# Eight experts on lists of chosen tokens instead of on all tokens: 55 tiles of 128 rows, gathered and scattered by DMA

## The chip, the core and the metric

The kernel runs on one core of a Trainium2 chip. The metric is the device time of one execution in microseconds, the median of several runs; lower is better. The core's engines work side by side from their own instruction queues: TensorE (PE, with its weight loads listed apart as PEld), VectorE (DVE), ScalarE (ACT), GpSimd (POOL) and SyncE (SP). SP, ACT and POOL can start DMAs.

## The reference

Two blocks in a row, all in float32: a gated linear recurrence over 768 tokens for each of 4 x 8 heads of 48, and a router that sends each of the 3072 resulting rows x (384 wide) to its two best of eight experts.

```python
for t in range(S):
    state = alpha[:, :, t, :, None] * state + np.einsum('bhd,bhe->bhde', k[:, :, t], v[:, :, t])
    y[:, :, t] = np.einsum('bhd,bhde->bhe', q[:, :, t], state)
# x = y as (3072, 384)
noisy_logits = x @ w_gate + np.log1p(np.exp(x @ w_noise)) * noise
top2 = np.argpartition(-noisy_logits, 2, axis=1)[:, :2]      # weights top2_w: softmax over the two
for e in range(E):
    for k in range(2):
        mask = top2[:, k] == e
        h = np.maximum(x[mask] @ w1[e], 0.0)                  # w1[e]: 384 x 1024
        out[mask] += top2_w[mask, k, None] * (h @ w2[e])      # w2[e]: 1024 x 384
```

## The kernel before

**The recurrence.** The tokens are cut into 24 chunks of 128, six to a batch, and two neighbouring chunks (a pair) run in step. `gla_prepare` loads q, k, alpha and v of a chunk, turns the first three by TensorE transposes (L141, through the PSUM tile `tp`, copied out by ACT or DVE at L142) and forms the diagonal scores. Then seven levels follow (`gla_level`): each makes scores of 4 x 2 heads (`scores`, L148, into `sc`), which DVE copies through a mask into `MT` (L187), while DVE (L197), ACT (L198, L200) and POOL (L199 for `k_new`, L202 for `tot`) scale queries and keys for the next level. `gla_finish` turns the keys (L215), updates the state (L219, L223 to L227), forms y (L233, L238), copies it to `y_sb` (L241) and turns it into `xT` (L246, L247), in which the model dimension lies on the partitions.

**The router.** After every three chunks (a unit of 384 tokens, eight units) `router` makes the logits (L254), the noise, the two best experts and their weights, and writes a dense table `gates`: for each token and expert a weight, which is zero for six of the eight.

**The experts.** `expert(e, u)` runs expert e on all 384 tokens of unit u: eight groups of three matmuls of 384 columns give h (L292, into `h_ps`), ACT takes the Relu (L295), and for each of three chunks eight matmuls of 384 columns give `o_ps` (L301). DVE multiplies by the gate and adds into `acc`, which stays in SBUF for all tokens (L304, L306). The last expert's results go out from there (L308). So all 8 x 8 expert-units are computed, whether a token chose the expert or not. An expert's `w1` and `w2` are loaded once.

**The order.** The recurrence and the router stand under `tc.high_priority()`; expert 0 is written between the pairs and fills TensorE's gaps there. Experts 1 to 7 follow. PSUM has two buffers of each `sc`, one `tp`, one `y` and two for the experts.

## Time and profile before

| | us |
|---|---|
| median of 3 runs (lowest, highest) | 2685.22 (2683.45, 2692.03) |
| span of the profiled execution | 2681.0 |
| PE busy | 2601.9 (97%) |
| PEld, DVE, ACT, POOL busy | 1695.4, 436.9, 461.9, 202.2 |
| L292 and L301, busy | 1047.9 and 1032.3 |
| DMA | 50.52 MB, 19 GB/s on the mean |

The page gives no time outside the span for the profiled execution, so its own time is taken as its span; the median lies 4.2 us above it. Busy time is the union of the instructions' times. A float32 matmul stands in the trace as two instructions (and two weight loads), a transpose as one. An "idle before" names what ended the wait.

### The profile page before, as it was taken

What the parts mean: (1) busy time and instruction counts of PE and PEld (TensorE: products, weight loads), DVE (VectorE), ACT (ScalarE), POOL (GpSimd) and SP (SyncE); (2) the same over time, 40 slices, a digit from 0 to 9 for tenths busy, and PEclk for the clock granted to TensorE, in tenths of its full rate; (3) what the DMA queues carried; (4) which work ended last, traced back from release to release, by engine and by line L of the source; (5) the groups of instructions that cost most, each with busy time, mean ns of one, the idle gap of its engine ahead of it and who ended that gap; (6) DMA issues with size and microseconds to landing.
All of it is one profiled execution on the core that took longest, in us unless ns stands there. A gap on an engine that the chain in (4) does not pass through costs nothing.

```text
span 2681.0 us, 25489 instructions
## 1 busy us (share of the span) xinstructions
PE 2601.9 (97%) x10504; PEld 1695.4 (63%) x10504; DVE 436.9 (16%) x1012; ACT 461.9 (17%) x1005; POOL 202.2 (8%) x412
## 2 busy tenths in 40 slices
PE   7889898999999999999999999999999999999999
PEld 6767677767877655555555555555555555555555
DVE  4333234323544100000000000000000000000000
ACT  2222122222332111111111111111111111111111
POOL 3221022222222000000000000000000000000000
PEclk9975766577777999999999999999999999999999
DMA  7111001111100000010001000000100010000000
GB/s 155 24 21 25 9 19 21 25 24 25 25 16 1 24 24 0 0 47 0 0 0 48 0 0 16 32 0 0 47 0 0 0 48 1 0 1 9 21 21 21
DMA packets 118820, 50.52 MB, mean 19 GB/s; under 512 B 104368, under 2 KB 115632, under 8 KB 118704
## 3 DMA queue, kind: packets, MB, share of 16 engines
q1 hardware_dynamic: 114816, 48.77, 7.3%
q8 instruction: 83, 1.36, 0.2%
q10 hardware_dynamic: 3888, 0.12, 0.1%
q14 instruction: 33, 0.27, 0.0%
HBM read 44.16 MB, written 4.72 MB: 18 GB/s over the span
## 4 chain that ended last, share of the span: by engine, by line
PE 77%; ACT 1%; DVE 0%; issue 0%; ACTq 0%; DVEq 0%
PE h_ps L292 35%; PE o_ps L301 35%; PE sc L148 5%; PE y L238 1%; PE tp L141 1%; PE y L233 0%; PE s L219 0%; PE lg L254 0%; PE tp L215 0%; PE tp L246 0%; DVE q_new L197 0%; ACT L258 0%; DVE q L174 0%; DVE MT L171 0%; ACT tot L142 0%
## 5 line engine op out<-in xcount | busy, mean ns | idle before, releaser
L292 PE MATMUL h_ps<-xT,w 128*128 128x384 f32 x3072 | 1047.9, 498 | 1.7 <-ACT xT L247 1.7
L301 PE MATMUL o_ps<-w,h 128*128 128x384 f32 x3072 | 1032.3, 493 | 0.0
L292 PEld LDWEIGHTS h_ps<-xT,w 128*128 128x128 f32 x3072 | 589.0, 194 | 398.7 <-issue 10.5
L301 PEld LDWEIGHTS o_ps<-w,h 128*128 128x128 f32 x3072 | 583.2, 192 | 392.2 <-issue 4.1
L295 ACT ACTIVATE h<-h_ps 128x384 f32<-128x384 f32 x512 | 251.4, 491 | 1646.4 <-PE h_ps L292 1646.4
L306 DVE SCALAR_TENSOR_TENSOR acc<-o_ps,gates,acc 128x384 f32<-128x384 f32 x168 | 103.8, 618 | 1630.0 <-PE o_ps L301 1630.0
L148 PEld LDWEIGHTS sc<-q_new,k_new 48*128 48x128 f32 x2304 | 258.6, 320 | 51.6 <-issue 26.6
L148 PE MATMUL sc<-q_new,k_new 48*128 48x64 f32 x2304 | 271.3, 412 | 0.0
L187 DVE COPY_PREDICATED MT<-mask,sc 128x256 f32<-128x256 uint32 x336 | 155.0, 526 | 161.0 <-PE sc L148 158.5
L199 POOL TENSOR_TENSOR k_new<-k_new,tot 128x256 f32<-128x256 f32 x144 | 94.2, 656 | 210.0 <-PE sc L148 206.6
L200 ACT COPY k_new<-k_new 128x256 f32<-128x256 f32 x144 | 59.0, 410 | 165.7 <-PE sc L148 148.9
L202 POOL TENSOR_TENSOR tot<-tot 128x256 f32<-128x256 f32 (+6 forms) x168 | 59.8, 356 | 348.4 <-ACT tot L142 281.2
L148 PE MATMUL sc<-q,k 48*128 48x128 f32 (+1 forms) x768 | 75.9, 341 | 8.8 <-DVE MT L171 8.8
L148 PEld LDWEIGHTS sc<-q,k 48*128 48x128 f32 x768 | 69.8, 247 | 15.5 <-DVE MT L171 9.9
L238 PEld LDWEIGHTS y<-vt,MT 128*128 128x128 f32 x384 | 65.2, 256 | 6.3 <-PE s L219 2.3
L238 PE MATMUL y<-vt,MT 128*128 128x48 f32 x384 | 65.0, 333 | 1.9 <-DVE S_bd L223 1.9
L198 ACT COPY q_new<-q_new 128x256 f32<-128x256 f32 x144 | 58.2, 406 | 40.0 <-issue 19.0
L197 DVE TENSOR_TENSOR q_new<-q_new,tot 128x256 f32<-128x256 f32 x144 | 61.1, 439 | 0.0
L141 PE MATMUL tp<-ident,k_in 128*128 128x128 f32 x96 | 23.9, 381 | 20.5 <-DMA k_in<-in_k_dram 11.2
L219 PEld LDWEIGHTS s<-vt,k_end 128*128 128x128 f32 x160 | 30.3, 269 | 15.9 <-ACT k_end L216 11.0
L219 PE MATMUL s<-vt,k_end 128*128 128x96 f32 x160 | 32.0, 359 | 7.4 <-ACT k_end L216 7.4
L233 PE MATMUL y<-S_bd,q_new 128*128 128x96 f32 x160 | 29.6, 342 | 9.5 <-DVE S_bd L227 9.5
(63 smaller groups left out, 521.4 us busy)
## 6 DMA issues: line engine op xcount, KB each, us to landing
w<-in_moe_w_dram SPq DMA_DIRECT2D x16, 1536.0 KB, 6.9
a_in<-in_alpha_dram SPq DMA_DIRECT2D x24, 192.0 KB, 2.7
q_in<-in_q_dram SPq DMA_DIRECT2D x24, 192.0 KB, 2.7
k_in<-in_k_dram SPq DMA_DIRECT2D x24, 192.0 KB, 2.7
vt<-in_v_dram SPq DMA_DIRECT2D x24, 192.0 KB, 2.7
out_dram<-acc SPq DMA_DIRECT2D x24, 192.0 KB, 1.9
noise<-in_moe_noise_dram ACTq DMA_DIRECT2D x1, 96.0 KB, 7.4
w_r<-in_moe_w_gate_dram ACTq DMA_DIRECT2D x1, 12.0 KB, 3.2
```

The lines of the kernel that those rows point to most:

```text
L148: nc.tensor.matmul(sc[i][:, at + j * width:at + (j + 1) * width], kT[r, j, :], qcols[r, j], start=True, stop=True)
L187: nc.vector.copy_predicated(halves(MTs[n % 2][:, i], L)[1], masks[L], part)
L197: nc.vector.tensor_mul(qr_new, q_right, t_left.to_broadcast([C, NP * g, L]))
L199: nc.gpsimd.tensor_tensor(kl_new, k_left, t_right.to_broadcast([C, NP * g, L]), op=ALU.mult)
L200: nc.scalar.copy(kr_new, k_right)
L202: nc.gpsimd.tensor_tensor(tot_new.rearrange("p j g -> p (j g)")[:, :, None], t_left, t_right, op=ALU.mult)
L219: nc.tensor.matmul(s1[:, j], k_end[:, j, :], vt[:, 2 * j:2 * j + 2, :], start=True, stop=True)
L238: nc.tensor.matmul(y[:, h, :], MT[:, i, j, :], vt[:, h, :], start=first and h == 0, stop=h == H - 1, skip_group_check=True)
L292: nc.tensor.matmul(h_ps, w1[:, a, ds(fo * C, C)], xT[:, a, ds(u * UT, UT)], start=a == 0, stop=a == KO - 1)
L295: nc.scalar.activation(h, h_ps, AF.Relu)
L301: nc.tensor.matmul(o_ps, hT[fo][:, ds(c * C, C)], w2[:, fo, :], start=fo == 0, stop=fo == FO - 1)
L306: nc.vector.scalar_tensor_tensor(acc[:, n, :], o_ps, gate, acc[:, n, :], op0=ALU.mult, op1=ALU.add)
```

## The change

The recurrence computes what it did; its PSUM tiles `tp` and `y` get two buffers each, since the experts' PSUM tiles come later. Nothing of the experts is left in that stage. `gla_finish` now also stores each chunk's `y_sb` to DRAM (`x_rows`). `router` no longer writes `gates`: with two small matmuls against triangular and full matrices of ones it counts each token's place in its expert's list, and POOL scatters (token number, weight) pairs of 8 bytes into the DRAM `table` by six indirect DMAs a unit, 48 in all. `out` is set to zero by DMA.

After the recurrence the counts give a `plan`: for each of 55 tiles (48 full ones' worth of 6144 list entries plus 7 for the rounding up of eight lists) the expert and the first table row. The recurrence's pools are closed. Then for every tile SP reads two registers from `plan`, loads 128 table rows (`tab`) and that expert's whole `w1` (`fetch`, two tiles ahead), POOL gathers the 128 rows of x by an indirect DMA, TensorE turns them, h and `o_ps` follow with 128 tokens in place of 384 (TensorE reads the expert number to address `w2`, which lies in SBUF for all experts), POOL gathers the rows that `out` has so far (`prev`), DVE forms weight x o + prev, and POOL scatters the result back to `out`. A list's end is filled with a number beyond the last token, which the indirect DMAs skip.

```diff
+    RMAX = N
+    NTILE = (2 * N) // C + E - 1
+    TROWS = E * RMAX + (E + 0) * C
+    NONE = 2 * N
...
-    ps_sc = pool("ps_sc", 2, space=PS)
-    ps_tp = pool("ps_tp", 1, space=PS)
-    ps_y = pool("ps_y", 1, space=PS)
-    ps_e = pool("ps_e", 2, space=PS)
...
+    ps_sc = pool("ps_sc", 2, gla, space=PS)
+    ps_tp = pool("ps_tp", 2, gla, space=PS)
+    ps_y = pool("ps_y", 2, gla, space=PS)
...
+    x_rows = dram.tile([N, DM], F32, name="x_rows")
+    table = dram.tile([TROWS, 2], U32, name="table")
...
-    def load_expert(e):
-        w1 = w1p.tile([C, KO, F], F32, name="w1")
-        nc.sync.dma_start(out=w1, in_=moe_w1[e].rearrange("(a p) f -> p a f", p=C))
-        w2 = w2p.tile([C, FO, DM], F32, name="w2")
-        nc.sync.dma_start(out=w2, in_=moe_w2[e].rearrange("(a p) d -> p a d", p=C))
-        return w1, w2
...
+    w2 = const.tile([C, E, FO, DM], F32, name="w2")
+    def load_w2():
+        for e in range(E):
+            nc.sync.dma_start(out=w2[:, e], in_=moe_w2[e].rearrange("(a p) d -> p a d", p=C))
...
+        nc.scalar.copy(xT[:, :, ds(at * C, C)], tp[:, 0:KO, :])
+        nc.sync.dma_start(out=x_rows[ds(n * C, C), :], in_=y_sb)
...
+    def router(u, xT):
         lg = ps_y.tile([C, UC, 2, E], F32, tag="y", name="lg")
         for c in range(UC):
             for a in range(KO):
-                nc.tensor.matmul(lg[:, c], xT[:, a, ds((u * UC + c) * C, C)], w_r[:, a],
+                nc.tensor.matmul(lg[:, c], xT[:, a, ds(c * C, C)], w_r[:, a],
...
+        nc.gpsimd.tensor_copy(out=entry.bitcast(I32)[:, :, :, 0],
+                              in_=token[:, ds(u * UC, UC), None].to_broadcast([C, UC, 2]))
...
+        chosen = rp.tile([C, UC, E], F32, name="chosen")
+        nc.vector.tensor_add(chosen, picked[:, 0], picked[:, 1])
+        past = rp.tile([C, UC, E], F32, name="past")
+        nc.vector.tensor_copy(out=past[:, 0], in_=seen[u % 2])
+        for c in range(1, UC):
+            nc.vector.tensor_add(past[:, c], past[:, c - 1], chosen[:, c - 1])
+        nc.vector.tensor_add(seen[(u + 1) % 2], past[:, UC - 1], chosen[:, UC - 1])
+        rank = ps_y.tile([C, UC, E], F32, tag="y", name="rank")
+        nc.tensor.matmul(rank, before, chosen, start=True, stop=False)
+        nc.tensor.matmul(rank, ones, past, start=False, stop=True)
...
+        place_u = rp.tile([C, 2 * UC], U32, name="place_u")
+        nc.vector.tensor_copy(out=place_u, in_=place_f)
         for c in range(UC):
-            n = u * UC + c
-            o_ps = ps_e.tile([C, DM], F32, tag="e", name="o_ps")
-            for fo in range(FO):
-                nc.tensor.matmul(o_ps, hT[fo][:, ds(c * C, C)], w2[:, fo, :], start=fo == 0, stop=fo == FO - 1)
-            gate = gates[:, n, e:e + 1]
-            if e == 0:
-                nc.vector.tensor_scalar(out=acc[:, n, :], in0=o_ps, scalar1=gate, scalar2=None, op0=ALU.mult)
-            else:
-                nc.vector.scalar_tensor_tensor(acc[:, n, :], o_ps, gate, acc[:, n, :], op0=ALU.mult, op1=ALU.add)
-            if e == E - 1:
-                nc.sync.dma_start(out=out[ds(n * C, C), :], in_=acc[:, n, :])
-    # ---- the recurrence, two chunks in step, and the router go first; the first expert fills their gaps ----
-    weights = None
+            for k in range(2):
+                i = k * UC + c
+                nc.gpsimd.indirect_dma_start(
+                    out=table, out_offset=bass.IndirectOffsetOnAxis(ap=place_u[:, i:i + 1], axis=0),
+                    in_=entry.bitcast(U32)[:, c, k, :], in_offset=None)
...
     for n in range(0, NT, 2):
-        with tc.high_priority():
-            pair = {m: gla_prepare(m) for m in (n, n + 1)}
-            for L in LEVELS:
-                for m, c in pair.items():
-                    gla_level(m, c, L)
+        pair = {m: gla_prepare(m) for m in (n, n + 1)}
+        for L in LEVELS:
             for m, c in pair.items():
-                gla_finish(m, c)
+                gla_level(m, c, L)
+        for m, c in pair.items():
+            if m // UC not in xTs:
+                xTs[m // UC] = xtp.tile([C, KO, UT], F32, name="xT")
+            gla_finish(m, c, xTs[m // UC], m % UC)
         if n == 0:
             load_router()
-            weights = load_expert(0)
+            for i in range(8):
+                nc.sync.dma_start(out=out.rearrange("(i n p) d -> i p n d", i=8, p=C)[i], in_=zeros)
+        if n == 2:
+            load_w2()
         while (done + 1) * UC <= n + 2:
-            with tc.high_priority():
-                router(done)
-            expert(0, done, *weights)
+            router(done, xTs.pop(done))
             done += 1
-    for e in range(1, E):
-        weights = load_expert(e)
-        for u in range(NU):
-            expert(e, u, *weights)
...
+    total = ps_y.tile([C, E], F32, tag="y", name="total")
+    nc.tensor.matmul(total, ones, seen[NU % 2], start=True, stop=True)
+    total_sb = rp.tile([1, E], F32, name="total_sb")
+    nc.vector.tensor_copy(out=total_sb, in_=total[0:1, :])
...
+    plan = const.tile([1, NTILE, 2], I32, name="plan")
+    nc.vector.tensor_copy(out=plan[:, :, 0], in_=of)
+    nc.vector.tensor_copy(out=plan[:, :, 1], in_=first)
...
+    def fetch(i):
+        e = nc.values_load(plan[0:1, i, 0:1], engines=[mybir.EngineType.SP], min_val=0, max_val=E - 1,
+                           skip_runtime_bounds_check_because=WHY)
+        r = nc.values_load(plan[0:1, i, 1:2], engines=[mybir.EngineType.SP], min_val=0, max_val=TROWS - C,
+                           skip_runtime_bounds_check_because=WHY)
+        tab = tp_.tile([C, 2], U32, name="tab")
+        nc.sync.dma_start(out=tab, in_=table[ds(r, C), :])
+        w1 = w1p.tile([C, KO, F], F32, name="w1")
+        nc.sync.dma_start(out=w1, in_=moe_w1[ds(e, 1)].rearrange("o (a p) f -> p (o a) f", p=C))
+        nc.gpsimd.indirect_dma_start(out=x_in[i % NB], out_offset=None, in_=x_rows,
+                                     in_offset=bass.IndirectOffsetOnAxis(ap=tab[:, 0:1], axis=0),
+                                     bounds_check=N - 1, oob_is_err=False)
+        return tab, w1
+    def ffn(i, tab, w1):
+        e = nc.values_load(plan[0:1, i, 0:1], engines=[mybir.EngineType.PE], min_val=0, max_val=E - 1,
+                           skip_runtime_bounds_check_because=WHY)
+        x_ps = ps_x.tile([C, KO, C], F32, name="x_ps")
+        for a in range(KO):
+            nc.tensor.transpose(x_ps[:, a, :], x_in[i % NB][:, ds(a * C, C)], ident)
+        xt = xp.tile([C, KO, C], F32, name="xt")
+        nc.vector.tensor_copy(out=xt, in_=x_ps)
+        h = hp.tile([C, FO, C], F32, name="h")
+        for half in range(2):
+            h_ps = ps_h.tile([C, FO // 2, C], F32, name="h_ps")
+            for fo in range(FO // 2):
+                for a in range(KO):
+                    nc.tensor.matmul(h_ps[:, fo, :], w1[:, a, ds((half * FO // 2 + fo) * C, C)], xt[:, a, :],
+                                     start=a == 0, stop=a == KO - 1)
+            nc.scalar.activation(h[:, ds(half * FO // 2, FO // 2), :], h_ps, AF.Relu)
+        o_ps = ps_o.tile([C, DM], F32, name="o_ps")
+        for fo in range(FO):
+            nc.tensor.matmul(o_ps, h[:, fo, :], w2[:, ds(e, 1), fo, :].rearrange("p o d -> p (o d)"),
+                             start=fo == 0, stop=fo == FO - 1)
+        nc.gpsimd.indirect_dma_start(out=prev[i % 2], out_offset=None, in_=out,
+                                     in_offset=bass.IndirectOffsetOnAxis(ap=tab[:, 0:1], axis=0),
+                                     bounds_check=N - 1, oob_is_err=False)
+        o = op.tile([C, DM], F32, name="o")
+        nc.vector.scalar_tensor_tensor(o, o_ps, tab.bitcast(F32)[:, 1:2], prev[i % 2], op0=ALU.mult, op1=ALU.add)
+        nc.gpsimd.indirect_dma_start(out=out, out_offset=bass.IndirectOffsetOnAxis(ap=tab[:, 0:1], axis=0),
+                                     in_=o, in_offset=None, bounds_check=N - 1, oob_is_err=False)
+    ahead = [fetch(0), fetch(1)]
+    for i in range(NTILE):
+        if i + 2 < NTILE:
+            ahead.append(fetch(i + 2))
+        ffn(i, *ahead[i])
```

How the instructions now stand, at the places on which the prediction rests. TensorE in the expert stage before, from one unit's last h group through its three o groups (`w` are the weights, an entry is one float32 matmul or several alike):

```order
L292 MATMUL h_ps<-xT,w_8585 128x384 [waits Activation_49]
L292 MATMUL h_ps<-xT,w_8585 128x384 x2
L301 MATMUL o_ps<-w_8587,h 128x384 [waits Activation_49]
L301 MATMUL o_ps<-w_8587,h 128x384 x6
L301 MATMUL o_ps<-w_8587,h 128x384 [waits Activation_49]
L301 MATMUL o_ps<-w_8587,h 128x384 x8
L301 MATMUL o_ps<-w_8587,h 128x384 [waits DVE_49]
L301 MATMUL o_ps<-w_8587,h 128x384 x7
```

TensorE in the tile stage now, from the transposes of two tiles to the first o matmul of the first of them (TENSOR_LOAD reads the register, ISA forms the address):

```order
L429 MATMUL x_ps<-ident,x_in_5727 128x128 [waits DMASW6_49]
L429 MATMUL x_ps<-ident,x_in_5727 128x128 x2
L429 MATMUL x_ps<-ident,x_in_5728 128x128 [waits DMASW1_49]
L429 MATMUL x_ps<-ident,x_in_5728 128x128 x2
L437 MATMUL h_ps<-xt,w_9103 128x128 [waits DMAHW3_49,DVE_49]
L437 MATMUL h_ps<-xt,w_9103 128x128 x11
L437 MATMUL h_ps<-xt,w_9103 128x128 [waits PE_49]
L437 MATMUL h_ps<-xt,w_9103 128x128 x11
L425 TENSOR_LOAD plan
L442 ISA
L442 MATMUL o_ps<-w_189,h 128x384 [waits Activation_49]
L442 ISA
```

The transposes of two tiles stand together, ahead of the first one's h; the h of every second tile follows the o of the tile before it directly.

VectorE at the end of the program before, and in the tile stage now:

```order
L304 TENSOR_SCALAR acc<-o_ps,gates 128x384 [waits PE_49] x3
L304 TENSOR_SCALAR acc<-o_ps,gates 128x384 [waits DVE_49,PE_49]
L304 TENSOR_SCALAR acc<-o_ps,gates 128x384 [waits PE_49] x2
L306 SCALAR_TENSOR_TENSOR acc<-o_ps,gates,acc 128x384 [waits PE_49] x18
L306 SCALAR_TENSOR_TENSOR acc<-o_ps,gates,acc 128x384 [waits DVE_49,PE_49] x150
```

```order
L431 COPY xt<-x_ps 128x384 [waits DVE_49,PE_49] x2
L448 SCALAR_TENSOR_TENSOR o<-o_ps,tab,prev_5731 128x384 [waits DMASW7_49,DMASW3_49,DMAHW2_49,DVE_49,PE_49]
L448 SCALAR_TENSOR_TENSOR o<-o_ps,tab,prev_5730 128x384 [waits DMASW6_49,DMASW2_49,DMAHW4_49,DVE_49,PE_49]
L431 COPY xt<-x_ps 128x384 [waits DVE_49,PE_49] x2
L448 SCALAR_TENSOR_TENSOR o<-o_ps,tab,prev_5731 128x384 [waits DMASW5_49,DMASW1_49,DMAHW6_49,DVE_49,PE_49]
```

The two copies that TensorE's next h waits for stand behind the sum of the tile before, and that sum waits for a gather (DMASW).

POOL in the middle of a pair's levels before, and at the like place now (`tot` and `k_new` of two chunks alternate), then POOL in the tile stage, where before there was nothing:

```order
L199 TENSOR_TENSOR k_new<-k_new,tot_1749 128x128x2 [waits PE_49]
L199 TENSOR_TENSOR k_new<-k_new,tot_1769 128x128x2 [waits PE_49]
L199 TENSOR_TENSOR k_new<-k_new,tot_1787 128x64x4 [waits PE_49,Activation_49,Pool_49]
L199 TENSOR_TENSOR k_new<-k_new,tot_1805 128x64x4 [waits PE_49,Activation_49,Pool_49]
L199 TENSOR_TENSOR k_new<-k_new,tot_1825 128x32x8 [waits PE_49,Activation_49,Pool_49]
```

```order
L338 DMA table<-entry,place_u 25600x2 [waits DVE_49]
L224 TENSOR_TENSOR k_new<-k_new,tot_1674 128x128x2 [waits PE_49]
L224 TENSOR_TENSOR k_new<-k_new,tot_1694 128x128x2 [waits PE_49]
L338 DMA table<-entry,place_u 25600x2 [waits DMASW6_49]
L224 TENSOR_TENSOR k_new<-k_new,tot_1712 128x64x4 [waits PE_49,Activation_49,Pool_49]
L224 TENSOR_TENSOR k_new<-k_new,tot_1730 128x64x4 [waits PE_49,Activation_49,Pool_49]
```

```order
L449 DMA out_dram<-o,tab 3072x384 [waits DMASW4_49,DVE_49]
L444 DMA prev_5731<-out_dram,tab 128x384 [waits DMASW7_49,DMASW6_49]
L419 DMA x_in_5727<-x_rows,tab 128x384 [waits DMAHW6_49,PE_49]
L449 DMA out_dram<-o,tab 3072x384 [waits DMASW7_49,DVE_49]
L444 DMA prev_5730<-out_dram,tab 128x384 [waits DMASW2_49,DMASW1_49]
```

In the recurrence one scatter now stands between two levels, and each waits for the scatter ahead of it (DMASW). In the tile stage a tile's gather of `prev` waits for the scatter of the tile before, since both touch `out`.

## Rows read from the trace of the kernel before

**Rows 1.** The page: engine totals, PE in 40 slices, granted clock.

```profile
PE 2601.9 (97%) x10504; PEld 1695.4 (63%) x10504; DVE 436.9 (16%) x1012; ACT 461.9 (17%) x1005; POOL 202.2 (8%) x412
...
PE   7889898999999999999999999999999999999999
...
PEclk9975766577777999999999999999999999999999
```

**Rows 2.** Stretches: length, busy per engine (instructions), granted clock, DMA share, GB/s.

```profile
0.00:943.50 943.50, 868.00 (x5128) 674.16 (x5129) 332.49 (x843) 241.90 (x557) 202.17 (x412) 0.75 0.14 29
943.50:2681.00 1737.50, 1733.94 (x5377) 1021.25 (x5375) 104.40 (x169) 220.04 (x448) 0.00 (x0) 1.00 0.04 13
11.17:72.46 61.29, 52.74 (x350) 47.09 (x350) 24.70 (x54) 15.59 (x38) 15.95 (x30) 1.00 0.65 151
...
30.00:40.00 10.00, 10.00 (x95) 9.95 (x95) 7.42 (x18) 4.30 (x12) 3.89 (x6) 1.00 1.04 388
```

**Rows 3.** The page's groups: busy us, mean ns of one, idle before.

```profile
L292 PE MATMUL h_ps<-xT,w 128*128 128x384 f32 x3072 | 1047.9, 498 | 1.7 <-ACT xT L247 1.7
L301 PE MATMUL o_ps<-w,h 128*128 128x384 f32 x3072 | 1032.3, 493 | 0.0
```

**Rows 4.** Timeline of the last units: start, length, instruction, idle before.

```profile
2615.36 15.64 PE L292 MATMUL h_ps<-xT,w 128*128 128x384 f32 x48
...
2630.84 15.64 PE L301 MATMUL o_ps<-w,h 128*128 128x384 f32 x48
...
2646.32 15.64 PE L292 MATMUL h_ps<-xT,w 128*128 128x384 f32 x48
...
2677.48 0.62 DVE L306 SCALAR_TENSOR_TENSOR acc<-o_ps,gates,acc 128x384 f32<-128x384 f32 x1 [4.54 <-PE o_ps L301]
```

**Rows 5.** Timeline of the first two pairs, which run without expert work.

```profile
11.17 1.09 PE L141 MATMUL tp<-ident,k_in 128*128 128x128 f32 x4 [11.17 <-DMA k_in<-in_k_dram]
12.93 1.11 PE L141 MATMUL tp<-ident,q_in 128*128 128x128 f32 x4 [0.68 <-ACT k L142]
...
28.23 17.49 PE L148 MATMUL sc<-q_new,k_new 48*128 48x64 f32 x158
...
35.65 0.64 POOL L199 TENSOR_TENSOR k_new<-k_new,tot 128x256 f32<-128x256 f32 x1 [1.23 <-PE sc L148]
...
54.57 3.62 PE L238 MATMUL y<-vt,MT 128*128 128x48 f32 x16 [0.93 <-DVE S_bd L223]
...
60.32 1.09 PE L215 MATMUL tp<-ident,k_new 128*128 128x128 f32 x4 [0.66 <-ACT xT L247]
...
72.46 1.12 PE L141 MATMUL tp<-ident,k_in 128*128 128x128 f32 x4 [0.57 <-ACT xT L247]
...
123.45 17.27 PE L292 MATMUL h_ps<-xT,w 128*128 128x384 f32 x48 [0.57 <-ACT xT L247]
```

**Rows 6.** Timeline just behind the first expert work, through the first router.

```profile
150.88 0.60 PE L215 MATMUL tp<-ident,k_new 128*128 128x128 f32 x4
...
155.21 1.91 PE L238 MATMUL y<-vt,MT 128*128 128x48 f32 x16
...
157.69 2.18 PE L254 MATMUL lg<-w_r,xT 128*128 128x16 f32 x18 [0.57 <-ACT y_sb L241]
...
163.55 0.16 DVE L274 TENSOR_TENSOR den<-w 128x3 f32<-128x3 f32 x1 [0.16 <-ACT w L272]
```

**Rows 7.** DMA issues: instructions, KB each, median us from issue to landing.

```profile
w<-in_moe_w_dram SPq DMA_DIRECT2D x16, 1536.0 KB, 6.9
...
out_dram<-acc SPq DMA_DIRECT2D x24, 192.0 KB, 1.9
noise<-in_moe_noise_dram ACTq DMA_DIRECT2D x1, 96.0 KB, 7.4
```

**Rows 8.** All groups of instructions: the shortest kind on POOL.

```profile
L347 POOL MEMSET const-float32-1.0<- 128x1 f32 x1 | 0.1, 99 | 0.0
```

More of the change, by code (lines that the diff above doesn't have):

```diff
@@ L83 @@
         g = C // (2 * L)
-        m = const.tile([C, g, L], F32, name=f"mask{L}")
+        m = gc.tile([C, g, L], F32, name=f"mask{L}")
         nc.gpsimd.memset(m, 1.0)
@@ new lines @@
+    ends = rp.tile([1, E], F32, name="ends")
+    nc.vector.tensor_tensor_scan(ends, ones[0:1, 0:E], tiles, 0.0, op0=ALU.mult, op1=ALU.add)
+    behind = rp.tile([1, NTILE, E], F32, name="behind")
+    nc.vector.tensor_tensor(behind, tile_no[:, :, None].to_broadcast([1, NTILE, E]),
+                            ends[:, None, :].to_broadcast([1, NTILE, E]), op=ALU.is_ge)
+    of = rp.tile([1, NTILE], F32, name="of")
+    nc.vector.reduce_sum(out=of, in_=behind, axis=mybir.AxisListType.X)
+    nc.vector.tensor_mul(behind, behind, tiles[:, None, :].to_broadcast([1, NTILE, E]))
@@ new lines @@
+    for t in x_in + prev:
+        nc.gpsimd.memset(t, 0.0)
+    WHY = "computed from the counts, in range by construction"
+    def fetch(i):
[11 more added lines that the diff above has]
+        return tab, w1
```

120 lines of the change are left out of this document (79 added, 41 removed).

## The prediction

> **What bounds the kernel now.** I read the page's totals and slices first: TensorE is busy 97% of the span, without a gap in the last two thirds, while POOL is done after them [rows 1]. Then the stretches: the seven experts from 943.5 us on hold TensorE for 1733.9 of 1737.5 us at granted clock 1.00, with the DMA engines at 4% [rows 2]. The groups say whose time it is: L292 and L301 are 2080 us of the 2681 [rows 3]. The last units show that nothing else matters there: h and o follow each other every 15.48 us (2615.36, 2630.84, 2646.32), so one expert on one unit of 384 tokens is 30.96 us, and seven experts on eight units are 56 x 30.96 = 1734 us [rows 4]. That stage is pure matmul, and six of every eight token-expert pairs in it are multiplied by zero. The stage ahead of it, 943.5 us, is the recurrence with expert 0 in its gaps, at clock 0.75 on the mean.
>
> What the recurrence is by itself stands at the start, before any expert work is ready: the first pair goes from 11.17 to 72.46, 61.3 us, of which TensorE is busy 52.7 [rows 2, 5]. The granted clock reads 1.00 there, but no change of it is recorded yet, and the same work says otherwise: four transposes take 1.09 us in it and 0.60 just behind the first expert unit, the 16 matmuls of L238 3.62 and 1.91 [rows 5, 6]. So the recurrence alone runs at the lower level, 1.2 GHz, though TensorE is busy 10.00 of 10 us in its levels [rows 2]; expert work before it is what brought the higher one.
>
> **The change part by part. Removed:** all of expert 0 to 7 on all tokens, 64 x 30.96 = 1981 us of full-clock TensorE time.
>
> **Stage one, the recurrence without expert work.** Three pairs of a batch: 61.3 us; 63.1 (72.46 to 123.45, and a second finish like 60.32 to 72.46 behind it); about 58.7 for the third, whose last chunk has no state to update (transposes 1.09, matmuls and two waits, some 4.4 in all) [rows 5]. That is 183 a batch, 732 for four. The second buffers of `tp` and `y` take away the waits for one buffer: 0.68 and its like twice a chunk, 0.93, 0.66 and 0.57 in the finish [rows 5]; the first pair's idle time is 61.3 - 52.7 = 8.6, and I count 5.5 of it as gone, 66 in all. With the 11.2 us before the first transpose: 677. The work that could hide in those gaps (expert 0) is gone, so nothing is won or lost by it beyond this.
>
> The router comes on top. The logits, 2.18 us at the higher level [rows 6], are about 4.1 at the lower; two counting products are four instructions more, about 0.9; and TensorE meets a wait for the chain of ACT and VectorE, which took from 157.69 + 2.18 to 163.55, 3.7 us, to the sum of the weights [rows 6], behind which the list of chosen experts now stands. TensorE's order has other work ahead of the counting product at most boundaries; I take 2 of it. Eight units x 7 = 56: stage one 733.
>
> 48 scatters now stand in POOL's queue between the `k_new` of one level and the next; queued behind each are the keys that TensorE's next scores need. POOL waits 1.23 us for TensorE ahead of each 0.64 us of `k_new` [rows 5], twice a level, so one scatter of up to 2.4 us in a level is covered by that wait. No row shows an indirect DMA. Its nearest rows are the store of 192 KB in the same 1536-byte rows, 1.9 us to landing, and, as the costliest for its size, 96 KB in 3072 pieces, 7.4 us [rows 7]. At 1.9 the scatters are free; at 7.4, each waiting for the one before, 48 x 5 = 240 us. I take 0.4 us each, 19: stage one ends at **752** (bounds 733 and 973).
>
> **Between the stages** one thing follows another: 6 us from the last logits through places and counts; six scatters in a row, each waiting for the one before (3 us each, 18; bounds 11 and 44); the table rows, then the gather beside the first `w1`, 6.9 us [rows 7], 9; transposes and copy, 2. Sum **35** (28 to 61). TensorE has stood still by then, so the first tile starts at the lower level: **4** more.
>
> **Stage two, 55 tiles.** An o product has the same eight matmuls of 384 columns as before, a third of 15.48: 5.16 us [rows 4]. The h product has 24 matmuls of 128 columns in place of 384. By columns that is 5.16; but each instruction also loads 128x128 weights, and where the columns are few (48) the pitch is 1.91 / 16 = 0.119 us [rows 6], by which 48 instructions would be 5.7. I take 5.4. Three transposes are 3/4 of 0.60, 0.45 [rows 6]. Sum 11.0.
>
> Two waits come on top. For every second tile, the copies of two turned tiles stand on VectorE behind the sum of the tile just finished: 0.62 for the sum [rows 4] and about as much for the copy, 0.4 in hand-offs, less the 0.9 of transposes that run meanwhile: 0.7, or 0.4 a tile. And the register with the expert number is read between h and o. No row shows such a read; it lies between nothing (the queue behind it still busy) and the 1.9 us of the shortest transfer [rows 7]; 0.8, nearer to nothing, since a read moves 4 bytes. A tile is 12.2 us, 55 are **671** (bounds 11.0 and 14.0: 605 and 770). The Trainium skill's page DMA: Bandwidth & Descriptors (Latency and other measured facts) gives such a read a floor of about 600 ns; by that the stage would be 11 us shorter, 660, which no run here shows yet.
>
> What hides the DMAs: the sum of one tile must be scattered before the next tile's `prev` may be gathered, and that must land before the next sum. From sum to sum this chain is 0.6 + scatter + gather; at 3.5 us each (nearer to the 1.9 us row, as it has the same rows and bytes, but with software descriptors and beside the loads of `w1`) it is 7.6, under the 11.4 to 12.9 us that TensorE needs from one o to the next: 3.8 us of cover, gone when a transfer passes 5.4. The gather of x is issued two tiles ahead. `w1` now comes 55 times, 1536 KB each with 6.9 us to land [rows 7], some 1.5 tiles ahead; with three row transfers of 192 KB that is 2.16 MB in 12.2 us, 177 GB/s, where 388 were reached [rows 2]. **The tail**: a last sum and scatter, 4.
>
> Sum: 752 + 35 + 4 + 671 + 4 = 1466, and 4 us by which the median lies above the span: **1470 us**.
>
> **The rivals.** *The chain through `out` sets the tile.* If an indirect transfer is nearer to the 7.4 us of many pieces [rows 7], from sum to sum it is 0.6 + 7.4 + 7.4 + 0.4 = 15.8, TensorE waits in every tile, and stage two is 869; with 50 more for the scatters in stage one and 26 more between the stages, about 1740. For it: 128 pieces each, generated by POOL, beside 16 engines' worth of `w1`; against: half the bytes' rows are as long as those of the 1.9 us store.
>
> *The tiles run at 1.2 GHz.* TensorE then needs about 2 x 11.0 + 1.2 = 23.2 a tile, 1276, in all about 2075. For it: the levels of the recurrence are all busy and stay at the lower level. Against: 128 rows by 128 and 384 columns are the experts' own kind of work, which holds 1.00 for 1737 us [rows 2], and the waits I find are about 1 us.
>
> *The recurrence gets the higher level.* Its TensorE work would halve, to 26 us a pair, the waits stay: 35 x 12 + 11 + 45 = 476 in place of 752, about 1195 in all. Rows speak against it: two pairs of it alone, 112 us, stayed at the doubled durations [rows 5]. The Trainium skill's page TensorE: Matmul & The Clock Gate (Part 1) has it that sustained matmul activity releases the throttle, and by that rule this case would come; the durations here disagree for TensorE work of this kind, at least before.
>
> *Slower: POOL writes the row addresses one by one.* If each of 128 rows costs about what POOL's shortest instruction takes, 99 ns [rows 8], an indirect transfer holds POOL for 12.7 us, three make a tile 38 us, and stage two is 2096; the 48 scatters, 10 us each beyond their cover, add 490 to stage one: about 3340. It decides from 165 transfers and 48 scatters reaching the 1890 us between 795 and 2685, that is from about 9.4 us each, 73 ns a row. Against it: the nearest row with many pieces, 3072 in 7.4 us [rows 7], is 2.4 ns a piece.
>
> *The change doesn't do what it says*, in that the 55 tiles are fixed: the seven for rounding cost full price (already in the sum, 85 us) and cannot cost more.
>
> **How the numbers follow.** Forecast, tiles set by TensorE at the higher clock: 0.62, with its own range 1400 to 1600 (bounds of register read, scatters and the middle). Chain through `out`: 0.22, 1600 to 1850, mostly below 1760. Tiles at 1.2 GHz: 0.07. Recurrence at 2.4 GHz: 0.05. Slower: 0.02; the rest scatters. The range to hold 8 in 10 is 1370 to 1760. A change under 0.3% is about what a measurement of this kernel can't tell from none: faster 0.97, same 0.01, slower 0.02.
>
> **What the profile after would show.** Right: a recurrence that ends near 750 us, its L173 at the durations of [rows 5]; 55 tiles at a pitch of 12 us with o at 5.2 and h at 5.4; granted clock 1.00 in them; VectorE's sum waiting for TensorE, not for a DMA. Wrong: the sum waiting for `prev` (the chain), h at twice 5.4 (the clock), POOL busy through a tile (row by row), or a gap of over 60 us between the stages.

## The result, and the profile after

The changed kernel takes 1466.8 us (median; 1463.9 to 1474.7) where the kernel before takes 2688.0; the ratio is 0.5464, 95% interval 0.5446 to 0.5482. The forecast was 1470 us. The profiled execution spans 1462.2 us, 4.6 less than the median.

From the page, first the totals, then the span in 40 slices (36.6 us each), as in [rows 1]:

```profile
PE 1241.1 (85%) x8079; PEld 1071.5 (73%) x8079; DVE 394.7 (27%) x985; ACT 274.5 (19%) x603; POOL 425.4 (29%) x653
...
PE   6895697997979979699850999989999989999896
...
PEclk8655555555555555555555999999999999999999
```

TensorE's busy time has gone from 97% to 85%, and the two stages are plain to see: the recurrence at half clock (0.5, the lower level of 1.2 GHz) up to slice 21, one slice in which TensorE does almost nothing, then the tiles at full clock. The stretches have the columns of [rows 2]:

```profile
10.05:755.60 745.55, 629.78 (x4394) 585.22 (x4394) 325.42 (x852) 208.60 (x493) 242.19 (x425) 0.55 0.25 55
...
755.00:800.00 45.00, 0.64 (x4) 0.55 (x3) 4.67 (x18) 0.00 (x0) 9.19 (x9) 0.50 0.17 61
...
800.02:1451.25 651.23, 611.30 (x3685) 486.23 (x3685) 61.92 (x110) 65.67 (x110) 163.62 (x161) 0.99 0.49 173
```

So the time is 755.6 + 44.4 + 651.2 + 11.0 us for the recurrence, the middle, the tiles and the tail, against 752 + 35 + 675 + 4 (671 and the 4 of the first tile) in the prediction. What TensorE waits for shows where its 15% went (waiting engine and line, releaser: us in all, times, longest):

```profile
PE x_ps L429 <- DMA x_in<-x_rows,tab: 81.8, 26, 44.4
PE sc L173 <- POOL k_new L224: 41.4, 13, 20.8
PE tp L240 <- POOL k_new L224: 31.1, 6, 8.7
...
PE h_ps L437 <- DVE xt L431: 1.7, 3, 0.7
```

In the recurrence TensorE waits 72.5 us (41.4 and 31.1) for keys (`k_new`) that stand on POOL behind the table scatters; 20.8 of it is one wait, behind the first unit's scatters. In the tiles it waits 37.4 us (81.8 less the 44.4 of the middle) for the gather of x. The scatters' own groups say why the keys are late:

```profile
L338 POOL DMA_INDIRECT table<-entry,place_u x48 | 48.7, 1015 | 176.9 <-DMA table<-entry,place_u 106.2
```

```profile
L338 POOL DMA_INDIRECT table<-entry,place_u x48: 957/1006/1364, 123.0 to 785.6; - x48
...
DMA to landing us min/median/max: 4.5/5.2/9.0
```

POOL spends 1.0 us on each, and each waits until the one before has landed (its data has arrived), 5.2 us from its issue on the median. The middle is a row of six of them, from the timeline (start, us, what, idle time before and its releaser):

```profile
755.07 0.57 PE L366 MATMUL total<-seen,ones 128*128 128x8 f32 x2
...
756.95 1.36 POOL L338 DMA_INDIRECT table<-entry,place_u  x1 [30.04 <-DVE ends L376]
...
763.32 0.96 POOL L338 DMA_INDIRECT table<-entry,place_u  x1 [5.00 <-DMA table<-entry,place_u]
...
785.59 0.96 POOL L338 DMA_INDIRECT table<-entry,place_u  x1 [4.58 <-DMA table<-entry,place_u]
790.41 0.36 SPq L416 DMA_DIRECT2D tab<-table  x1
...
800.02 0.90 PE L429 MATMUL x_ps<-ident,x_in 128*128 128x128 f32 x3 [44.37 <-DMA x_in<-x_rows,tab]
...
801.62 8.21 PE L437 MATMUL h_ps<-xt,w 128*128 128x128 f32 x48 [0.70 <-DVE xt L431]
```

Two tiles on TensorE and the start of the next two, as [rows 4] showed the units before. The order is the transposes of two tiles, then the two tiles; 23.49 us for two (1008.64 to 1032.13), 11.84 a tile on the mean of 55:

```profile
1006.50 0.49 PE L429 MATMUL x_ps<-ident,x_in 128*128 128x128 f32 x3
1008.26 0.55 PE L429 MATMUL x_ps<-ident,x_in 128*128 128x128 f32 x3 [1.27 <-DMA x_in<-x_rows,tab]
1008.64 5.52 PE L437 MATMUL h_ps<-xt,w 128*128 128x128 f32 x48
1014.00 5.33 PE L442 MATMUL o_ps<-w,h 128*128 x16
1019.17 5.52 PE L437 MATMUL h_ps<-xt,w 128*128 128x128 f32 x48
1024.52 5.33 PE L442 MATMUL o_ps<-w,h 128*128 x16
1029.69 0.49 PE L429 MATMUL x_ps<-ident,x_in 128*128 128x128 f32 x3
1031.75 0.55 PE L429 MATMUL x_ps<-ident,x_in 128*128 128x128 f32 x3 [1.57 <-DMA x_in<-x_rows,tab]
1032.13 5.52 PE L437 MATMUL h_ps<-xt,w 128*128 128x128 f32 x48
```

An h is 5.36 us from its start to that of o, an o 5.17 to the next h: 10.53 a tile. The gather of x costs 1.27 and 1.57 before every second tile. Two waits, of SP and of POOL, lead to it:

```profile
SPq L416 <- DMA out_dram<-o,tab: 504.7, 52, 23.4
...
POOL x_in L419 <- DMA tab<-table: 59.8, 44, 3.9
```

SP may load the next table rows only when a scatter of sums has landed, and POOL waits for these rows before it issues the gather. Behind the scatter issued at 1020.27 the table rows follow at 1023.09, the gather at 1025.54, the transposes at 1031.75. These are the second tile's transposes, which TensorE's order has ahead of the first tile's products: the rows of x are needed a whole tile before the second tile's own h. No run here tries the other order.

### The profile page after: what moved, and what is told of

Its sections match the earlier page's. It is cut to its first block, busy times and chain, and to the rows that moved or that the text cites. A ratio compares the mean times of both kernels' runs of the same rounds, so it can differ in the third digit from the quotient of the medians.

```text
span 1462.2 us, 21684 instructions
## 1 busy us (share of the span) xinstructions
PE 1241.1 (85%) x8079; PEld 1071.5 (73%) x8079; DVE 394.7 (27%) x985; ACT 274.5 (19%) x603; POOL 425.4 (29%) x653
## 5 line engine op out<-in xcount | busy, mean ns | idle before, releaser
L437 PEld LDWEIGHTS h_ps<-xt,w 128*128 128x128 f32 x2640 | 308.5, 196 | 10.1 <-DVE xt L431 2.9
L437 PE MATMUL h_ps<-xt,w 128*128 128x128 f32 x2640 | 311.3, 279 | 1.8 <-DVE xt L431 1.7
L173 PE MATMUL sc<-q_new,k_new 48*128 48x64 f32 x2304 | 268.2, 418 | 42.0 <-POOL k_new L224 41.4
L173 PEld LDWEIGHTS sc<-q_new,k_new 48*128 48x128 f32 x2304 | 257.9, 327 | 53.0 <-POOL k_new L224 44.6
L442 PE MATMUL o_ps<-w,h 128*128 x880 | 292.9, 486 | 0.0
L442 PEld LDWEIGHTS o_ps<-w,h 128*128 128x128 f32 x880 | 163.2, 190 | 101.8
L448 DVE SCALAR_TENSOR_TENSOR o<-o_ps,tab,prev 128x384 f32<-128x384 f32 x55 | 34.0, 618 | 559.7 <-PE o_ps L442 496.3
L439 ACT ACTIVATE h<-h_ps 128x512 f32<-128x512 f32 x110 | 65.7, 597 | 626.7 <-PE h_ps L437 626.7
L449 POOL DMA_INDIRECT out_dram<-o,tab x55 | 56.4, 1026 | 306.7 <-DVE o L448 294.4
L338 POOL DMA_INDIRECT table<-entry,place_u x48 | 48.7, 1015 | 176.9 <-DMA table<-entry,place_u 106.2
L429 PE MATMUL x_ps<-ident,x_in 128*128 128x128 f32 x165 | 28.9, 287 | 81.8 <-DMA x_in<-x_rows,tab 81.8
L444 POOL DMA_INDIRECT prev<-out_dram,tab x55 | 56.4, 1026 | 112.3 <-DMA out_dram<-o,tab 108.6
L419 POOL DMA_INDIRECT x_in<-x_rows,tab x55 | 54.8, 996 | 79.4 <-DMA tab<-table 59.8
```

The source lines that it names most:

```text
L173: nc.tensor.matmul(sc[i][:, at + j * width:at + (j + 1) * width], kT[r, j, :], qcols[r, j], start=True, stop=True)
L419: nc.gpsimd.indirect_dma_start(out=x_in[i % NB], out_offset=None, in_=x_rows, in_offset=bass.IndirectOffsetOnAxis(ap=tab[:, 0:1], axis=0), ...
L437: nc.tensor.matmul(h_ps[:, fo, :], w1[:, a, ds((half * FO // 2 + fo) * C, C)], xt[:, a, :], start=a == 0, stop=a == KO - 1)
L439: nc.scalar.activation(h[:, ds(half * FO // 2, FO // 2), :], h_ps, AF.Relu)
L442: nc.tensor.matmul(o_ps, h[:, fo, :], w2[:, ds(e, 1), fo, :].rearrange("p o d -> p (o d)"), start=fo == 0, stop=fo == FO - 1)
L444: nc.gpsimd.indirect_dma_start(out=prev[i % 2], out_offset=None, in_=out, in_offset=bass.IndirectOffsetOnAxis(ap=tab[:, 0:1], axis=0), bou ...
```

## The experiments

Each changes the kernel after. Stages are read from its profiled run: up to the start of the product that counts the entries (`total`), from there to the first turned tile, to the end of the last sum, and from there to the end (the tail). Stage one of the same code came out between 755 and 767 us in seven kernels (762 on the mean, and 755.1 in the changed kernel is the shortest), the tiles of the same code between 641 and 652, so a difference under 10 us in one stage of one run says little.

| kernel | median, us | ratio to before, interval | stage one | middle | tiles | tail |
|---|---|---|---|---|---|---|
| after | 1466.8 | 0.5446 to 0.5482 | 755.1 | 44.9 | 651.2 | 11.0 |
| expert 0's register | 1465.8 | 0.5442 to 0.5476 | 764.4 | 44.7 | 642.1 | 11.0 |
| single PSUM buffers | 1530.1 | 0.5694 to 0.5718 | 830.9 | 45.0 | 641.5 | 11.0 |
| six tables | 1391.8 | 0.5179 to 0.5198 | 714.5 | 24.3 | 637.2 | 11.0 |
| deeper fetch | 1448.0 | 0.5384 to 0.5402 | 758.1 | 45.6 | 632.4 | 11.0 |
| deeper, copies on ScalarE | 1439.3 | 0.5326 to 0.5378 | 764.4 | 44.7 | 616.3 | 10.9 |
| deeper, two gathers | 1584.5 | 0.5867 to 0.5917 | 766.6 | 44.0 | 766.2 | 6.8 |
| deeper, ScalarE, two gathers | 1500.1 | 0.5568 to 0.5596 | 760.4 | 44.6 | 691.5 | 6.9 |
| deeper, six tables | 1377.2 | 0.5111 to 0.5138 | 706.2 | 24.9 | 633.8 | 11.0 |
| deeper, six tables, ScalarE | 1370.8 | 0.5080 to 0.5115 | 712.6 | 23.8 | 622.1 | 10.9 |
| scores over 64 rows | 1461.7 | 0.5427 to 0.5461 | 755.7 | 44.0 | 646.9 | 11.0 |
| scores over 128 rows | 1481.7 | 0.5488 to 0.5549 | 780.7 | 43.7 | 651.0 | 11.0 |
| no last scatter | 1464.8, one run | none | 763.4 | 44.8 | 652.1 | 2.7 |

**The register read.**

```diff
-        e = nc.values_load(plan[0:1, i, 0:1], engines=[mybir.EngineType.PE], ...
+        e = 0
...
-            nc.tensor.matmul(o_ps, h[:, fo, :], w2[:, ds(e, 1), fo, :]...
+            nc.tensor.matmul(o_ps, h[:, fo, :], w2[:, e, fo, :],
```

> TensorE reads no register: every tile takes the second product's weights from expert 0 (a part of the computation that is changed), all else is as in the changed kernel. By the prediction's term, 0.8 us a tile, the time falls by 44 us to 1423. By the trace, where the read takes 0.30 us while the queued products of h still run and o starts 5.36 us after h without a gap, nothing changes: within 4 us of 1467.

1465.8 us: no change. (Its tiles, 642.1, are as long as the 641.5 of the kernel with single buffers, which reads the register.) The read, in the changed kernel (min/median/max ns, first and last start):

```profile
L425 PEldq TENSOR_LOAD <-plan x55: 299/303/489, 807.7 to 1443.3; - x55
```

0.30 us while the queued products of h still run: an o starts 5.36 us after its h, as steadily as the next h after the o. The prediction's 0.8 a tile, 44 us, was put on a read that the queued products cover. The Trainium skill's page DMA: Bandwidth & Descriptors (Latency and other measured facts) has a floor of about 600 ns for such a read, twice what this trace shows; since the read is hidden, neither figure counts here.

**The second PSUM buffers.**

```diff
-    ps_tp = pool("ps_tp", 2, gla, space=PS)
-    ps_y = pool("ps_y", 2, gla, space=PS)
+    ps_tp = pool("ps_tp", 1, gla, space=PS)
+    ps_y = pool("ps_y", 1, gla, space=PS)
```

> The PSUM pools for turned tiles and for sums have one buffer each again, as before the change. By the prediction's term, 5.5 us a pair, the time rises by 66 us to 1533. By the idle time of the first pair, 8.6 us before and 4.4 after, it is 4.2 a pair, 50 us, less what the scatters' waits swallow: 1500 to 1517.

1530.1 us, 63 more. By the traces it is 76 more in stage one (69 against the mean of the seven kernels) and 10 less in the tiles, whose code is the same. The prediction's 66 is about right, its mechanism only in part; the 1500 to 1517 us from idle time alone were too low. The recurrence with single buffers, to be read against the first stretch above (745.55 us, TensorE busy 629.78):

```profile
10.05:831.50 821.45, 674.55 (x4394) 609.46 (x4394) 326.57 (x854) 208.88 (x493) 238.17 (x425) 1.00 0.21 50
```

(The clock column reads 1.00 as in [rows 2]: no change is recorded in this stretch; durations are those of the lower level, 423 ns on the mean for the score products read from `q` and `k`, where the changed kernel has 333.) Of 76 us, 31 are waits (146.9 against 115.8 us idle). The other 45 are the same 4394 instructions running longer (against the mean of the seven, 28 and 41). In the changed kernel the end of one pair and the preparation of the next stand close together on TensorE, and there the granted clock goes up for a few microseconds, once in most pairs:

```profile
446.10:450.00 3.90, 3.90 (x30) 3.14 (x30) 1.14 (x2) 1.65 (x3) 0.34 (x1) 0.67 0.64 153
450.00:454.60 4.60, 3.69 (x44) 3.07 (x44) 4.03 (x8) 2.59 (x6) 3.90 (x10) 1.00 0.99 165
...
460.00:470.00 10.00, 9.95 (x94) 9.80 (x93) 6.82 (x18) 4.46 (x14) 4.85 (x8) 0.50 0.01 2
```

With single buffers TensorE waits some 0.9 us between the steps of that block (21.7 us in 24 waits for the copy of `k`, 17.2 in 20 for that of `q`), and the higher level doesn't come: the durations there stay those of the lower one.

**The 48 table scatters.** Six tables, so that no scatter waits for another:

```diff
-    table = dram.tile([TROWS, 2], U32, name="table")
+    tables = [dram.tile([TROWS, 2], U32, name=f"table{i}") for i in range(6)]
...
-                    out=table, out_offset=...
+                    out=tables[i], out_offset=...
...      the filling of the empty tables, now behind the first pair:
-    nc.scalar.dma_start(out=table...
+            for t in tables:
+                nc.scalar.dma_start(out=t...
...
-        tab = tp_.tile([C, 2], U32, name="tab")
-        nc.sync.dma_start(out=tab, in_=table[ds(r, C), :])
+        six = tp_.tile([C, 6, 2], U32, name="six")
+        for s in range(6):
+            nc.sync.dma_start(out=six[:, s], in_=tables[s][ds(r, C), :])
+        tab = tp_.tile([C, 2], U32, name="tab")
+        nc.vector.tensor_reduce(out=tab[:, 0:1], in_=six[:, :, 0], op=ALU.min, axis=...)
+        nc.vector.tensor_reduce(out=tab.bitcast(F32)[:, 1:2], in_=six.bitcast(F32)[:, :, 1], op=ALU.max, axis=...)
```

> Six tables in place of one, one for each of the six scatters of a unit, so that no scatter has to wait for the one before; a tile reads its rows from all six and takes the smallest row number and the largest weight. Theory (a scatter takes 5.2 us to land, and as each waits for the one before on POOL, the keys of the next levels stand behind them; the waits of TensorE for these keys were 72.5 us): stage one falls from 754 to 690 to 710 us, and between the stages six scatters take 6 + 5 us in place of 34, so that gap falls from 45 to 22 to 26; the time is 1375 to 1405. Rival (POOL's own time for 48 scatters, 1.0 us each, and the work of landing are what costs): stage one stays above 730, only the gap shrinks, 1430 to 1445.

1391.8 us, inside the theory's range: stage one 714.5, a little above what it gave, the middle 24.3. What is left of the waits for keys (with 6.9 us "issue" in the same group):

```profile
PE sc L172 <- POOL k_new L223: 13.4, 4, 7.7
...
PE sc L172 <- issue: 6.9, 4, 2.8
```

```profile
142.96 0.51 POOL L249 TENSOR_TENSOR S_bd<-S_bd,tot 48x192 f32<-48x192 f32 x1 [7.23 <-DMA table<-entry,place_u]
```

The longest, 7.7 us, stands in the first unit, where POOL waits 7.2 us for the scatters to land before it scales the state (`S_bd`). Most of the rest is POOL's own time: six scatters of 1.0 us follow each other directly. The three kernels with six tables have stage one at 706 to 715 us (711 on the mean, against 762 for the seven with one table), so the chain of scatters costs about 50 us there and 20 of the 45 in the middle.

**The gather of x.** First the fetch three tiles ahead, then also the copies on ScalarE:

```diff
-    tp_ = pool("tabp", 3)
+    tp_ = pool("tabp", 5)
-    NB = 3
+    NB = 5
-    ahead = [fetch(0), fetch(1)]
+    ahead = [fetch(0), fetch(1), fetch(2)]
-            ahead.append(fetch(i + 2))
+            ahead.append(fetch(i + 3))
...  second kernel:
-        nc.vector.tensor_copy(out=xt, in_=x_ps)
+        nc.scalar.copy(xt, x_ps)
```

> Three to five buffers for the gathered rows and for the table rows, and the rows of a tile fetched three tiles ahead in place of two. The changed kernel's trace has TensorE wait 37 us in stage two for the gather of x (81.8 us in 26 waits, less the 44.4 before the first tile), about 1.5 us before every second tile. Theory (the table rows have only three buffers, so the gather of a tile starts when the sum of the tile three before it has landed, and comes just too late): these waits go, stage two falls from 651 to about 615 us, the time to 1425 to 1437. Rival (the waits come from POOL's order, each gather standing behind the scatter and the gather of the tile in hand): within 10 us of 1467.

> The deeper fetch, and the copies of the turned rows on ScalarE in place of VectorE. With the deeper fetch alone (1448 us) TensorE no longer waits for the gather of x but 22.2 us for these copies, which stand behind the sum on VectorE. Theory: they need not stand there; the wait falls below 8 us, the time to 1428 to 1436. Rival (the hand-off costs as much from ScalarE, whose copy of the same tile is 0.5 us): within 5 us of 1448.

1448.0 us: half of the gain that was expected. The gather of x is no longer waited for in the tiles (45.0 us, the middle alone), and SP's wait of 504.7 us for the scatters is gone, as the theory has it; buffers and distance were changed together, so their shares are not told apart. But another wait shows that this one had covered, in the deeper-fetch kernel's group:

```profile
L437 PE MATMUL h_ps<-xt,w 128*128 128x128 f32 x2640 | 311.4, 279 | 22.2 <-DVE xt L431 22.2
```

These 22.2 us are the 0.4 a tile that the prediction had for the copies behind the sum on VectorE. With the copies on ScalarE they are 8.5 us and the tiles take 616.3, 35 less than after, where the two waits held 39. The time, 1439.3, misses the expected range by 3 us (in the profiled run stage one is 6 us longer than with the deeper fetch alone); the interval (0.5326 to 0.5378) lies below that of the deeper fetch alone.

**The chain through `out`.** On top of each of the last two kernels, `prev` is gathered twice:

```diff
         nc.gpsimd.indirect_dma_start(out=prev[i % 2], out_offset=None, in_=out, ...)
+        nc.gpsimd.indirect_dma_start(out=prev[i % 2], out_offset=None, in_=out, ...)
```

> On top of the deeper fetch: the rows of the output so far are gathered twice for each tile, the second after the first, which lengthens the chain from one sum to the next by one transfer. Counted from the changed kernel's trace that chain is 0.9 us to the scatter's issue, 3.1 to the gather's, 3.8 to its landing, 7.8 in all, and with the second gather 11.9 us. TensorE needs about 11.1 a tile with the deeper fetch. Theory (the chain stands hidden with some 3 us of cover, as the prediction has it): the chain now just sets the tile, 0.8 us more each, 44 us above the kernel with the deeper fetch alone, and VectorE's sum waits for the gather in most tiles. Rival (the chain never mattered, and a doubled gather overlaps the first): no change, under 5 us.

> As the run before it, with the rows of the output so far gathered twice. With the copies on VectorE the second gather cost 136 us. Theory (a late gather holds up the sum, the copies behind it on VectorE, and so TensorE for 2.8 to 5.6 us before every second tile, and after the longer ones TensorE runs at the lower level for a while; the chain itself is only some 12 us long): with the copies elsewhere the sum may be late, and the second gather costs 0 to 50 us above the run before, its clock staying near 1.00 in stage two. Rival (the chain from sum to sum is itself 14 us with two gathers and sets the tile): 100 us or more above the run before.

With the copies on VectorE it costs 136.5 us, three times the theory's 44 and far from the rival's none. From that kernel's timeline:

```profile
1104.60 0.62 DVE L451 SCALAR_TENSOR_TENSOR o<-o_ps,tab,prev 128x384 f32<-128x384 f32 x1 [13.33 <-DMA prev<-out_dram,tab]
1105.14 1.01 DVE L431 COPY xt<-x_ps 128x384 f32<-128x384 f32 x2
...
1105.74 8.47 PE L437 MATMUL h_ps<-xt,w 128*128 128x128 f32 x48 [4.49 <-DVE xt L431]
...
1119.21 5.52 PE L437 MATMUL h_ps<-xt,w 128*128 128x128 f32 x48
```

The late gather holds the sum, the sum holds the copies queued behind it, the copies hold TensorE for 4.49 us, and the 48 products behind that take 8.47 us where 5.52 is usual. The stretches name the reason, granted clock 0.50 behind the wait:

```profile
1100.40:1105.70 5.30, 0.85 (x7) 0.58 (x5) 1.10 (x3) 0.00 (x0) 1.20 (x2) 0.93 0.39 140
1105.70:1109.00 3.30, 3.26 (x15) 3.26 (x16) 0.45 (x1) 0.00 (x0) 2.51 (x3) 0.50 0.24 76
```

Over the tiles TensorE's busy time is 649.0 us against 609.6 with one gather, and it waits 116.5 us for the copies. With the copies on ScalarE the second gather costs 60.8 us (75 in the tiles): above the theory's 50, below the rival's 100. The rival's mechanism is what the trace shows, only with a shorter chain: 53 of 55 sums wait for `prev`, and TensorE waits 54.6 us for the sums to free the PSUM buffers of o. The chain then sets the tile, and can be read in that kernel's waits and timeline:

```profile
PE o_ps L442 <- DVE o L451: 54.6, 34, 5.7
...
1211.06 0.62 DVE L451 SCALAR_TENSOR_TENSOR o<-o_ps,tab,prev 128x384 f32<-128x384 f32 x1 [12.45 <-DMA prev<-out_dram,tab]
1211.96 1.03 POOL L452 DMA_INDIRECT out_dram<-o,tab  x1 [4.12 <-DVE o L451]
1213.29 1.03 POOL L419 DMA_INDIRECT x_in<-x_rows,tab  x1 [0.30 <-issue]
1214.81 0.99 POOL L444 DMA_INDIRECT prev<-out_dram,tab  x1 [0.48 <-DMA out_dram<-o,tab]
1218.62 1.00 POOL L447 DMA_INDIRECT prev<-out_dram,tab  x1 [2.82 <-DMA prev<-out_dram,tab]
1222.86 0.62 DVE L451 SCALAR_TENSOR_TENSOR o<-o_ps,tab,prev 128x384 f32<-128x384 f32 x1 [11.18 <-DMA prev<-out_dram,tab]
```

From sum to sum 11.8 us, of which the extra gather is 3.8 (1214.81 to 1218.62); 12.6 on the mean of 55 (691.5 / 55). So with one gather the chain is 8.0 to 8.8 us.

**The clock of the recurrence.** The score products read more rows:

```diff
-                r = ds(DP * i, D)
+                r = ds(DP * i, DP)        # second kernel: ds(0, C)
                 nc.tensor.matmul(sc[i][:, at + j * width:at + (j + 1) * width], kT[r, j, :], qcols[r, j],
```

> The score products read 64 rows of keys and queries in place of 48; the 16 more hold zeros, so the same is computed in as many instructions of as many columns. Theory (the 48-row products of 64 columns are what holds TensorE at the lower level, and a third more rows is too little): granted clock in the levels 0.50, time within 1% of 1467. Rival (a little more work in the array suffices): clock 1.00 in the levels, stage one 100 to 200 us shorter.

> The score products read all 128 rows, so the two heads that share a tile are summed into one another and the result is another one; instructions and columns stay as many. Theory (few rows keep the lower level): the granted clock in the levels rises to 1.00, the pitch of the level products falls from 0.115 us, and stage one from 754 to 560 to 640 us, bounded then by VectorE and POOL. Rival (rows don't matter, the waits or the small columns do): clock 0.50 in the levels and the time within 1% of 1467.

With 64 rows the recurrence runs as before, mean granted clock 0.55, as that theory has it. With 128 rows the mean goes up, and the time doesn't fall, it rises by 15 us:

```profile
10.05:781.20 771.15, 689.26 (x4394) 667.09 (x4394) 343.80 (x852) 209.40 (x493) 242.18 (x425) 0.72 0.23 53
```

Score products of 64 columns, over 128 rows at the granted clocks 0.51 and 1.00, then over 48 rows in the changed kernel at 0.50:

```profile
421.06 13.79 PE L173 MATMUL sc<-q_new,k_new 128*128 128x64 f32 x64 [1.62 <-POOL k_new L224]
...
474.05 6.21 PE L173 MATMUL sc<-q_new,k_new 128*128 128x64 f32 x54
```

```profile
456.77 17.72 PE L173 MATMUL sc<-q_new,k_new 48*128 48x64 f32 x157
```

An instruction (a float32 product has two) takes 0.215 us at the lower level and 0.115 at the higher one over 128 rows, and 0.113 at the lower one over 48 rows. So of the theory for 128 rows the clock came true for part of the stage (mean 0.72), the 560 to 640 us did not (780.7): a product over 128 rows costs at the higher level what one over 48 costs at the lower. Which raised the mean, the number of rows or what they hold, is not shown: the 16 rows that the first kernel adds are all zeros, of the 80 that the second adds 48 hold data.

**The tail.** The last tile's scatter is left out:

```diff
+        if i < NTILE - 1:
             nc.gpsimd.indirect_dma_start(out=out, out_offset=..., in_=o, ...)
```

> The changed kernel without the scatter of its last tile, whose rows are left as they were (a part of the computation left out). In the changed kernel 11 us lie between the last sum and the end, 10 of them POOL's drain, where 3.5 lay before. Theory (the drain waits for the last scatter): the end follows the last sum in 4 us or less. Rival (ending a program that has used POOL's software descriptors costs this much): still 8 to 11 us after the last sum.

The end does follow the last sum in 2.7 us, as the theory has it, but not for its reason: POOL's drain is as long as ever and has only begun earlier, behind a gather. After, and without the last scatter:

```profile
L482 POOLq DRAIN  x3: 45/107/10065, 1451.3 to 1461.9; - x3
```

```profile
L483 POOLq DRAIN  x3: 45/107/9992, 1452.2 to 1462.7; - x3
```

In the two kernels with a second gather it is 5.9 us. What sets its length stays open.

**Both.** The deeper fetch and the six tables, then with the copies on ScalarE:

> The deeper fetch and the six tables together. If their gains lie in different stages they add: stage one 690 to 710, gap 22 to 26, stage two 615: 1335 to 1370 us. If the six reads of table rows and their two reductions on VectorE come back as waits ahead of the sums, stage two stays near 651 and the time is 1375 to 1405.

> Deeper fetch, six tables, and the copies on ScalarE. Theory (the 22.6 us for which TensorE waits for these copies in the kernel with six tables and the deeper fetch go, and the lower level that follows the longer of them): 1350 to 1362 us. Rival (the six reads and their two reductions on VectorE are what comes late, by way of the row numbers): within 5 us of 1377.

1377.2 us, in the second range, although the tiles (633.8) do not stay near 651. The gain of the fetch shrinks from 19 to 15: with six tables and the old fetch TensorE waited for the gather of x only 20 us in the tiles (43.8 less the 23.7 of the middle), where the changed kernel waits 37, so less was left to gain. The copies are waited for 22.6 us, as with the deeper fetch alone (22.2). With the copies on ScalarE 1370.8 (interval 0.5080 to 0.5115), 6.5% under the changed kernel and the fastest of these; expected were 1350 to 1362. Its wait for the copies is down to 12.5 us, but the tiles still take 622.1, where they took 616.3 without the six tables; one run of each doesn't tell whether that is the reductions.

## Why the prediction was right

The sum came within 4 us, and that is in part luck: the stages were off by +4, +9, -24 and +7 us, and single terms by up to 53, with both signs.

**Stage one, 755.6 for 752.** Two misses that cancel. The recurrence and the router without scatters were 733, measured 683 (755.6 less 72.5 of waits for keys). A plain pair with its logits takes 55.7 us (446.08 to 501.82). The step that failed is "the recurrence alone runs at the lower level": it holds for the levels, 0.50 with TensorE busy 9.95 of 10 us, not for the block between two pairs, and that is worth the 41 to 45 us that single buffers lose again. The first pair shows it against [rows 2]: 52.28 us for 61.29, of which busy time is 4.8 and idle time 4.2 (the prediction counted 5.5 of idle time and nothing of busy time):

```profile
10.05:62.33 52.28, 47.91 (x350) 44.34 (x351) 24.61 (x54) 16.14 (x38) 18.08 (x38) 0.64 0.73 199
```

The scatters were 19, measured 72.5: the mis-sized step is the 0.4 us each, taken near to a plain store's 1.9 us [rows 7]. A landing of 5.2 lies nearer to the other end, 7.4, and the bounds (0 to 240) held it. With 5.2 the prediction's own formula, landing less 2.4 of cover, gives 48 x 2.8 = 134, so more was covered than it counts. That each scatter waits for the one before, and that the keys stand behind, was as told.

**The middle, 44.4 for 35.** The same price again: six scatters took 33.5 us (756.95 to 790.41), 5.6 each in place of 3. All else took 11 for 17.

**The tiles, 651.2 for 675.** h took 5.36 for 5.4 and o 5.17 for 5.16: for h the value taken between the 5.16 of the columns and the 5.7 of the 48-column pitch [rows 6] was right. TensorE's work is 611.3, 11.1 a tile, for 11.0. The first tile's lower level cost 2.7 us (8.21 for 5.52), forecast 4. Of the waits, 0.8 a tile for the register was nothing; the copies behind the sum were 22 us as forecast, but hidden (1.7) under a wait that the prediction hadn't, the gather of x, 37.4. The prediction said that this gather is issued two tiles ahead and left it there. It didn't ask when the buffers of the row numbers are free: `tab` has three, and a tile holds its own until its scatter has landed, so POOL waits for the next table rows (59.8 us) and the gather comes just too late for the second tile's transposes. The fixed number of tiles cost what was said; by the reference's own counts (748 to 822 entries an expert) 51 tiles hold rows and the last four are empty.

**The tail, 11 for 4.** POOL's drain, which no row of before shows.

**The rivals.** The chain through `out` never set the tile, as forecast: 49 of 55 sums wait for TensorE. Its length was put at 7.6 us; the doubled gather shows 8.0 to 8.8, a cover of some 3 us under the 11.84 of a tile. Transfers land in 5.8 (x), 3.8 (`prev`) and 2.6 us (the scatter of sums), about the 3.5 that was chosen. The tiles ran at 0.99. The recurrence got the higher level only between two pairs; in its levels TensorE is 99% busy at 0.50. The Trainium skill's rule that sustained matmul activity releases the throttle (TensorE: Matmul & The Clock Gate, Part 1) is not borne out by these stretches. POOL spends 1.0 us on an indirect transfer, a ninth of what the slower rival needed. (That rival's total is mis-added: 795, 2096 and 490 make about 3380, not 3340; nothing hangs on it.)

## What to carry to other kernels

Ask of every small scatter what it waits for: not the transfer's 1.0 us of POOL but the landing of the one before (5.2 us) was the price, and separate destinations took about 50 of 72 us away. When a buffer is prefetched, count back from the buffer that holds its address, not from the distance in the loop. And a wait that you remove may have covered another: the deeper fetch gave only half of the expected gain until the copies behind the sum were moved too.
